# Loading the first convolution's taps 0 and 4 in alternating column halves, with a new written-out order for every engine

## The chip, the cores and the metric

The kernel runs on 1 core of one Trainium2 chip. The metric is the device time of one execution in microseconds, the median of the runs shown. PE is the matmul engine, PEld its weight load, DVE the vector engine, ACT the scalar engine, POOL GpSimd, SP the engine that issues nearly all DMAs.

## What is computed

Two convolutions over time with five taps, each followed by gelu and by keeping every second step, then a joint of the result with a short second sequence. Shapes: x is 2 x 4000 x 512, each tap is 512 x 512, g is 2 x 8 x 512, the output is 2 x 1000 x 8 x 512, all bf16.

```python
for i in range(5): h = h + einsum("btc,cd->btd", xp[:, i:i+T, :], w1[i])
h = gelu(h)[:, ::2, :]
for i in range(5): f = f + einsum("btc,cd->btd", hp[:, i:i+T1, :], w2[i])
f = gelu(f)[:, ::2, :]
fe = einsum("btd,de->bte", f, w_f);  ge = einsum("bud,de->bue", g, w_g)
j = tanh(fe[:, :, None, :] + ge[:, None, :, :])
out = einsum("btud,dv->btuv", j, w_o)
```

## The kernel before

**Stages.** The channels lie on the partitions in four blocks of 128. The first 396 steps of h are made by the plain method ("direct"): for each tap in the order 0, 4, 2, 1, 3 and each of four output blocks m, four matmuls of 396 columns add into bank m of PSUM, 80 matmuls in all. Their x comes by two ordinary loads (xr) and a transposition on PE; DVE and ACT copy the result to xs, rows 0 and 2 of a group of four first (taps 0, 4 and 2 need only these), rows 1 and 3 by a second pair of copies (taps 1 and 3). The rest of h, and all of f, is made by units (class Unit, steps s1 to s5; class Triple, steps d, r, t, s). A unit computes three output steps at a time with fewer products, from sums and differences of rows of x (tiles row and xq or xp, on DVE and ACT) and from sums of taps (w1part for the first convolution, w2part for the second). The x of the units comes by transposing DMAs. Then follow the feature product (class Feature) and the joint: tanh on ACT into jT and jX, and products with w_o in groups of four tiles (class Seven) with seven products of half size in place of eight, from sums of j (tile ss, on DVE or POOL) and of w_o (tile tw). Products are evicted by ACT or DVE to sn or og, added there, and stored by SP.

**The sums of taps.** w1part(m, "s") makes, for output block m (128 columns of each tap): t = w0 + w4, u = w0 + 4 w4, then u + 2 w2, t - w2 and t + w2, on DVE, the results scaled by 1/3 on ACT. For m = 0 and 2 it also makes the sum and the difference of taps 1 and 3 for two blocks at once. u goes into the product "t2", the first of a unit; t - w2 into "tm"; the difference of taps 1 and 3 into "sm". Blocks 0 and 1 lie in the first half of a tap's columns.

**The loads.** All on SP, in this order: the two xr; tap 0 as two column halves of 256 KB; taps 4, 2, 1 and 3 whole, 512 KB each. From tap 2 on, the issue of a load waits for the landing of an earlier one (list came): tap 2 for the first xr, tap 1 for the second, tap 3 for tap 0's second half. Then come the transposing loads of x: xq[0] in the phases 4, 0, 2, 1, 3, 5, then xq[1], then xp.

**The order.** The kernel is first recorded as a list of operations, numbered as they are recorded. ORDER gives for each engine the numbers of its operations in the order in which they are issued, two characters each. Some operations (evictions, sums in the joint and feature stages) can run on one of two engines ("flex"); the table in which the number stands decides. edges() works out which operation must wait for which; emit() issues each engine's list with the waits on semaphores. So the table, and not the order in the source, sets who runs before whom, and an engine waits at the first operation in its list that isn't ready.

**The old order's start, on DVE:** both copies to xs; u of block 1 and of block 0; t of block 0; the three operations that add tap 2 to these; then on in the same way through blocks 2 and 3, mixed with the row operations of the first units. The row difference for "t2" stands 11 places after the first operation that uses tap 2.

**The old order's end, on PE:** the first half of the last tile, the last product (p4) of the last group, the second half of the last tile. DVE evicts p4 and then the second half; ACT evicts the first half and issues both stores of the halves.

Of the kernel before, what the change touches and what calls it, by code (L numbers as in the profile page):

```python
# [63 lines left out]
class Op:  # L64
# [3 lines left out]
ALPHABET = "0123456789ABCDEFGHIJKLMNOPQRSTUVWXYZabcdefghijklmnopqrstuvwxyz_-"  # L68
ORDER = {
    "pe": (  # L70
        "0X0Y0Z0a0b0c0d0e0f0h0j0l0t0u0v0w0x0y0z0_0-1011121314151617182C2v191g1A2c2J1i1j2m2K2n2E2e2f2x2y2F2p362q372M2N33342j3O"
        "3P303J313K2k3H3X3t3U3R3S3h3i3Z4A3e3V3a3v3f413w3k3l4Y4K4L4244454o4a4C4D3_3-4b4N4i4y5L4l4O4H4j4m4v4I4z5V4f4q5p4w4r5N5W"
        "5O4g5z5_4-5r5s6L5S5T50606N6O6l616S6V5w6W5x7R6n6v6T6o5Y5Z6y6Y786Z6s6w7b7c7I7J7F6z7p7G6t7A837B7T7U7r7s7L7Y7M80817Z7z8A"
        "7_7e8D8T858E7f7w868V8d7x8e8W8B8m8a8t8r8b8n8-908u8g8h8o9F9G8G8H9Q9T8y8z8p9D9K929f9R9L9U939N9q9h9o9y9v9O9xA3ANA2A7A09j"
        "A9AiAjAEABAw9kAxAZAaAHAKB1AIALAfApAqAcB2BDAdAgBEB4B5BKBLBVAsAtB7BAB8BYBZBNBOBkBBBbBRBcBqBSBrBWBtBuC8BeBhBiBfCHC1CBC9"
        "ClCCCEC2CFBzCWCICTB_CUCaCXCbCmCoCpCrCKCLD5D6DFD2CuD3DJCsCeDKCvDVDBDCCfDWDSDTDPDQCxCyDuDMDnDNDcDoDdDjDkDvDfDgDxDyE4E5"
        "EEEZEFEaE1E2ETEUEOD_D-EPE_EtEuEBECEKELEfFCE-EcEdFDEWEXFOF4F2FFFGFWFXEwFxExFjFIFJFyFZFuFaFrFsFlFQFLFvFMGKFfFgGEGLGTG7"
        "GUG8F_F-GFG1GAGBGNGWGeGfGOGzGQGRGYGhGiGwGxH3GnHMH5GoHNH0GtGuG_HYHEH1HgHhHBHCHFHSHVHTHaHxI1HWHIHJI2HyHPHQHpIYHqH_H-IS"
        "IBICHjIxITHkI4IyIZIVI5IWIIIJIiIbIjJBIEIcIFJCJOJ1IlJPJ2I_I-ImJ4JRJ5IrJEIsJFJeJIJSJfJUJVJXJJJtJhJiJuJYJzJ_JwJxJnKMKNK0"
        "K7K8KAKEJoKFK1KPKBKcKVKdKQKSKWKTLKL0LLKzKfKwKtKgLQKxKuK_L1KlLRKmL7LTL8LaLbLALBLELpLFLNLULjLOLkLqMILyLzMOLsLtLvLdLeMJ"  # L80
        "MlM6MPLwM3M7M4MRMmMSMAMBMYMLMMMuMZMfM-MgN0MrNGMoMpMbMcMsNHMvNlNMNJNKN6NNN7N2N3NWNXNZNmNPOEOFNaNuNQNdNvN-O0NeNrNsOKOU"
        "NoOLONOVOnOHNpO6O7OhOOOiOoO2O3P8OIP9ObOkOxOyOcOXOqOYP2OlOrPBPEPCPZP3POPPO_O-PFPHPRPSPIPcQ0PdQ1PaPiPjPVPsPWPfPpPqQ9Pg"
        "PtQCQ3Q4QDPwPxQ6QAQ7QFQGQJQKQMQNQQQTQUQX"),
    "act": (
        "080k1o1s1L0m1N1R2S1Q1P1B1y2D1C1q1D1h2d1_1a1k2L2o1c1F2w2U1E2r2I2X2O353Q2W2Y2l383I2i3u3Y3B3T3N323j3p3D3W3n3g4B3o3m2-43"
        "4Z4M4S404p3d46545M3z4k4U4P4n534J4_4x525q654h5X4e5-4G6-516m6M5U5v67626X5y5a4u5K7S6U5R79705o6a717K6x6R7H6_7d6u5J7j5n6r"
        "847q7l7a7N6K6J7-8F7E828U7g5h6k8O6j7X8f7v897y8C8s6D8P918c8N976d8Z8x8I9J778i9E8q8_9M9S9V94999i9p9r9z9PA4ATAO9-A6AkAUAG"
        "ADAWAVAJAXC4AMB0A-AYBFCjB9Ba9nBPC7C6BXBlBvChCkCiCAC3C5CVDHDICnD7DGCODsDtDLD4CgA_FADXERCzESFoDeDwDhF8F9F6F7E6DrEQGJED"
        "EgEvFqFEFPFnF3FYFpEyGsFbFBINFmGrHtG9GIGCHuGgIMGXGjJrIQHOGvJMHvIvHDHiIPHzIOI3KqIRHlIUIzHwIwIaIkKLJDJ3InJsKKJGJNJgJWJj"
        "J-KIK9KpKrKCKeNjKULIKhKvK-LoL9NhLCKJLJNELrLnLfMKLxKsM8MnMHMaMGMjMtMdNIMkN4NCNYNnNbOGNFNDODOWOMNiOjNkOpOCOZPAOgOfP0PG"  # L90
        "PTPbQ2PrPhPuQEQ8QHQRQSQZ"),
    "dve": (
        "000g0i1m1J1I1n1M1K1O2Q1l1u2R1r1p1w1S1X1x1v1U1T1H1V1z1W1G1Y1Z1b1-1t2g1d2z2P2G2T2_2H1e1f2V2h2Z2b2a2t3L2s3M393q2u3C3A3b"
        "3E3F3c3x3G3r3s49474R3y4E4F4T4c484X4d4Q55574s4V564W5d4t5b665t5u5P645c5Q6b5G636A6P5k5E5f735H5F686p5g5I6Q5i5j696q5l6G72"
        "6C5m7Q6c6H746E7C6B7P7D7k7t7i7V7O7u6F6g7o7W7h6I766e6h756f877m7n886i8X8Y8k8Q8v8S8l8R9H9I8w9895968j9W9Y9a9g9c9X9Z9e9b9s"
        "9C9B9w9t9_9uA5A1A8AA9AARAFAC9l9mAyAPAbAzAQ9dAlASArB3AeAhB6BMBHBJAuBIBmBCBdBTBsBpBgBoC_CPCDBjCGB-CJCYCqCcCMCNCtCwE7Ep"
        "DZDDEqE8DREADUDODpDqDlDzErEhEiEGEbE3EVE0EnFSEmEMEeEYF0F5FHEoFVFkFzFKFtFRFNFhGMFwG0GVG2GGGPGSGZGyH8HcH4GpH6G-H2HZHGHU"
        "HbHKHXHRHrIDI0I8IfJ7I6IKIXIGJ8IgJQJ0IdJ6ItJTJaK4JbK6JKJvJyKOJZJpK2KGKRKXL4KaL6L-KbLMKyKnLSL2LcLGLVLPLlLuL_LZMWMUM2M5"
        "MQMxMCMNMhMTN1MqMwNLN8NONSNxNTOQNyNRNwO1NtNfNqO8NzO4OJOPOzOdOmPDP4PQOsPJPePLPlPMPmPNPXPkQ5PyQBQLQOQVQY"),
    "pool": (  # L100
        "01020304050n0o0p0q21200r0s5e8MAnAmBGAoBnCRC-D0CQCSDYDaD1EsDbEkE9EjFUFTElG3GaG4G5H9G6GbGcH7I7HAHdGdI9J9HeHfIeIhIAJAJc"
        "K3JdL3KYK5KZM0LWLXL5LYM1MVMXMyMzM_NUORNVOTN_OSOtOuOvOwPKPoPn"),
    "sp": (
        "0607090A0B0C0D0E0F0G0H0I0J0K0L0M0N0O0P0Q0R0S0T0U0V0W22232425262728292A2B58595A5B5C5D8J8K8LAvBQBUBwBxByC0CZCdD8D9DADE"
        "DiDmEHEIEJENEzF1FcFdFeFiGDGHGkGlGmGqHHHLHmHnHoHsIHILIoIpIqIuJHJLJkJlJmJqKDKHKiKjKkKoLDLHLgLhLiLmM9MDMEMFMeMiN5N9NANB"
        "NcNgO5O9OAOBOaOeP1P5P6P7PUPYPvPzP_P-QIQPQW"),
}


# [175 lines left out]
def bass_standalone__seq2seq_rnn_t_joint__speech_kernel(  # L285
# [19 lines left out]
    B, T, D = x.shape  # L305
# [15 lines left out]
    with ExitStack() as es:  # L321
        cur = [16512]

        def at(name, shape, dtype, offset=None):
            o = cur[0] if offset is None else offset
            b = Buf(nc, name, shape, dtype, o)
            if offset is None:
                cur[0] = (b.end + 31) // 32 * 32
            return b
# [3 lines left out]
        w1_sb = at("w1_sb", [K, NK, D], BF16)  # L333
# [52 lines left out]
        pl = Plan(nc)  # L386
# [42 lines left out]
        def load_w(eng, dst, src):  # L429
            return pl.dma(eng, lambda e: e.dma_start(dst.ap, src), (), (dst,))  # L430
# [3 lines left out]
        def load_xr(rt):  # L434
            n = NR[rt]
            dst = xr[rt].rows(0, n).map(lambda a: a.rearrange("p r k c -> p (r k c)"))
            src = x[0, 4 * P * rt:4 * (P * rt + n), :].rearrange("(p r) c -> p (r c)", r=4)
            return pl.dma("sp", lambda e: e.dma_start(dst.ap, src), (), (dst,), nbytes=n * 4 * 2 * D)  # L438

        def load_x6(buf, b, ph, j0, col, n=336):  # L440

            r0 = b * T + 6 * j0 + ph
            dst = buf[ph, :, col:col + n]
            src = x.rearrange("b t d -> (b t) d")[r0:r0 + 6 * (n - 1) + 1:6, :]
            pl.dma("sp", lambda e: e.dma_start_transpose(out=dst.ap, in_=src), (), (dst,), nbytes=n * 2 * D, rate=172e3)

        came = [load_xr(rt) for rt in range(2)]
        act(warm[0:1], warm[1:2], ACT.Gelu_apprx_tanh)

        def load_w1(i):  # L450
            src = w1[i].rearrange("(k c) d -> c k d", c=P)
            if len(came) == 2:
                h = D // 2
                for sl in (slice(0, h), slice(h, D)):
                    o = pl.dma("sp", lambda e, sl=sl: e.dma_start(w1_sb[i, :, sl].ap, src[:, :, sl]), (), (w1_sb[i, :, sl],), nbytes=262144)  # L455
            else:
                o = load_w("sp", w1_sb[i], src)
                if len(came) > 3:
                    o.after.append(came[-4].idx)
            came.append(o)  # L460

        def load_xq(i, ph):
            load_x6(xq[i], 0, ph, 2 * NA // 3 + i * N3 - 2, 0, -(-(N3 + 3 - i) // 16) * 16)

        for kind, i in (('w', 0), ('w', 4), ('w', 2), ('w', 1), ('w', 3), ('x', 4), ('x', 0), ('x', 2), ('x', 1), ('x', 3), ('x', 5)):
            if kind == "w":
                load_w1(i)
            else:
                load_xq(0, i)
        for ph in (4, 0, 2, 1, 3, 5):  # L470
            load_xq(1, ph)
        for ph in (4, 0, 2, 1, 3, 5):
# [10 lines left out]
        for rt in range(2):  # L483
            for pp in range(2):
# [9 lines left out]
                o = xs[0][pp::2, :, 16 + rt * P:16 + rt * P + n]  # L494
# [187 lines left out]
        for m in range(NK):  # L682
            src = ps.pair(m * NT, NA, NA).map(lambda a: a.rearrange("p s (q r) -> p s r q", r=3))
            o = hT[0][:, m, HOFF:HOFF + NA // 3].map(lambda a: a.rearrange("p (r s) q -> p s r q", s=2))
# [516 lines left out]
```

## Time and profile before

| | us |
|---|---|
| median of 3 runs (250.22 to 250.87) | 250.55 |
| the profiled execution: device time | 250.92 |
| the profiled execution: span, first to last instruction | 249.10 |
| busy: PE, DVE, ACT, POOL | 242.8, 225.0, 210.4, 86.5 |
| first matmul of the 80 direct ones | 7.21 |
| first sum of taps on DVE | 9.48 |
| last matmuls begin | 244.94 |
| granted TensorE clock, mean | 1.000 |

The span is shorter than the device time by 1.82 us, which lie outside of the program's instructions. A row of the timeline is: start, time that the merged instructions span, engine, line, operation, output and inputs, shapes, count, and in brackets the idle time of the engine before it with what ended it. Matmuls overlap: one of 268 columns is shown with 0.28 us, but the next begins 0.115 us after it. Idle time of PE is therefore read from the starts. A row of the table by stretch is: stretch, length, busy time of PE, PEld, DVE, ACT and POOL with the number of instructions, granted clock, busy share of the DMA engines and GB/s.

### The profile page before, as it was taken

The numbers are of one execution on the slowest core, as the hardware profiler recorded it, in microseconds if no ns is written. First come the engines' busy times: TensorE is split into PE (matmuls) and PEld (weight loads), VectorE is DVE, ScalarE is ACT, GpSimd is POOL, SyncE is SP. The second block draws the span as 40 slices with busy tenths as digits, with TensorE's granted clock in tenths as the row PEclk, the third lists the DMA queues.
The fourth block names the chain that finished last, engine by engine and source line by source line (L and its number), as shares of the span: only waits on it lengthen the run. The fifth ranks groups of instructions, "written<-read, shape, count | busy, mean of one in ns | idle before, by whom it ended". The sixth has DMA issues, their size and how long they took to land.

```text
span 249.1 us, 5276 instructions
## 1 busy us (share of the span) xinstructions
PE 242.8 (97%) x1932; PEld 184.2 (74%) x1932; DVE 225.0 (90%) x399; ACT 210.4 (84%) x359; POOL 86.5 (35%) x92
## 2 busy tenths in 40 slices
PE   7999999999999999999999999999999999999994
PEld 3556888877666666666568887878778888888783
DVE  1599988984999999799999898999999999999994
ACT  2198699859765957996999999999999999999972
POOL 1000000000000000000015494677987796787850
PEclk9999999999999999999999999999999999999999
DMA  7999999985700620000000533223323665446557
GB/s 194 340 190 167 203 174 202 167 130 168 234 21 3 184 69 3 0 3 3 0 0 3 168 101 112 84 88 127 132 87 105 201 199 171 141 157 206 168 183 227
DMA packets 57323, 31.85 MB, mean 128 GB/s; under 512 B 33786, under 2 KB 57098, under 8 KB 57298
## 3 DMA queue, kind: packets, MB, share of 16 engines
q1 hardware_dynamic: 57010, 31.39, 48.0%
q8 instruction: 15, 0.25, 0.4%
q10 hardware_dynamic: 288, 0.13, 0.2%
q14 instruction: 10, 0.08, 0.1%
HBM read 7.64 MB, written 16.38 MB: 96 GB/s over the span
## 4 chain that ended last, share of the span: by engine, by line
PE 87%; DVE 7%; DMA 3%; issue 1%; SPq 1%; DVEq 0%
PE acc L412 87%; DMA w_sb<-in_w_dram 3%; DVE ssum L502 2%; DVE row L398 2%; DVE ssum L398 1%; DVE og L818 1%; DVE og L398 1%; DVE w_t L398 0%; SPq L455 0%; SPq L438 0%; DVE ss L886 0%; DVEq L321 0%; DVE w_x L398 0%; DVEq L246 0%
## 5 line engine op out<-in xcount | busy, mean ns | idle before, releaser
L398 DVE TENSOR_TENSOR og<-acc,sn 128x512 bf16<-128x512 f32 x93 | 59.6, 682 | 1.9 <-PE acc L412 1.6
L412 PE MATMUL acc<-tw,ss 128*128 128x256 f16 x372 | 57.6, 273 | 0.1
L404 ACT ACTIVATE jT<-feT,geT 128x1000 bf16<-128x1000 f32 (+6 forms) x56 | 52.1, 982 | 0.1
L817 ACT ACTIVATE sn<-acc 128x512 f32<-128x512 f32 (+1 forms) x67 | 41.3, 666 | 1.7 <-PE acc L412 1.6
L412 PEld LDWEIGHTS acc<-tw,ss 128*128 128x128 f16 x372 | 35.8, 98 | 6.4 <-DVE ss L886 0.4
L886 POOL TENSOR_TENSOR ss<-jT 128x512 f16<-128x512 bf16 x25 | 28.8, 1163 | 24.5 <-ACT jT L404 24.5
L412 PE MATMUL acc<-row,w_sb 128*128 128x334 bf16 (+1 forms) x192 | 32.0, 296 | 0.0
L412 PE MATMUL acc<-row,w_x 128*128 128x268 bf16 (+1 forms) x192 | 28.8, 291 | 0.5 <-ACT sd L404 0.4
L412 PE MATMUL acc<-wo_sb,jT 128*128 128x256 bf16 x176 | 28.9, 272 | 0.0
L404 ACT ACTIVATE sd<-acc 128x334 f32<-128x334 f32 (+1 forms) x48 | 20.1, 432 | 9.4 <-PE acc L412 7.3
L394 POOL MEMSET hT<- 128x8 bf16 (+2 forms) x6 | 0.7, 147 | 77.1 <-ACT hT L404 72.2
L404 ACT ACTIVATE jX<-feT,geT 128x1000 bf16<-128x1000 f32 (+4 forms) x28 | 27.0, 999 | 0.1
L412 PEld LDWEIGHTS acc<-row,w_x 128*128 128x128 bf16 x192 | 18.5, 98 | 6.9 <-ACT sd L404 0.7
L412 PEld LDWEIGHTS acc<-row,w_sb 128*128 128x128 bf16 x192 | 18.5, 98 | 6.5 <-DVE row L398 0.2
L412 PE MATMUL acc<-wo_sb,ss 128*128 128x256 bf16 x124 | 21.4, 273 | 0.0
L404 ACT ACTIVATE hT<-acc 128x268 bf16<-128x268 f32 (+2 forms) x36 | 15.0, 436 | 6.1 <-PE acc L412 6.1
L412 PEld LDWEIGHTS acc<-wo_sb,jT 128*128 128x128 bf16 x176 | 17.2, 98 | 2.9
L818 DVE COPY sn<-acc 128x512 f32<-128x512 f32 (+1 forms) x28 | 18.7, 679 | 0.1
L886 POOL TENSOR_TENSOR ss<-ss,jT 128x512 f16<-128x512 f16 x11 | 13.4, 1221 | 12.7 <-DVE ss L886 10.0
L412 PE MATMUL acc<-row,w_t 128*128 128x334 bf16 x96 | 17.0, 305 | 0.0
L817 ACT ACTIVATE og<-acc 128x512 bf16<-128x512 f32 x25 | 16.7, 668 | 0.2 <-PE acc L412 0.2
L412 PE MATMUL acc<-hT,w_sb 128*128 128x334 bf16 x96 | 16.8, 305 | 0.0
(115 smaller groups left out, 499.9 us busy)
## 6 DMA issues: line engine op xcount, KB each, us to landing
out_dram<-og SPq DMA_DIRECT2D x47, 256.0 KB, 2.3
w_sb<-in_w_dram SPq DMA_DIRECT2D x9, 512.0 KB, 5.9
out_dram<-og SPq DMA_DIRECT2D x15, 128.0 KB, 2.4
xr<-in_x_dram SPq DMA_DIRECT2D x1, 512.0 KB, 4.0
w_sb<-in_w_dram SPq DMA_DIRECT2D x2, 256.0 KB, 5.5
wf_sb<-in_w_f_dram SPq DMA_DIRECT2D x1, 512.0 KB, 3.6
wg_sb<-in_w_g_dram SPq DMA_DIRECT2D x1, 512.0 KB, 4.7
wo_sb<-in_w_o_dram SPq DMA_DIRECT2D x1, 512.0 KB, 5.7
```

Source lines behind the costliest of these rows:

```text
L394: pl.op("pool", lambda e: e.memset(v.ap, 0.0), (), (v,))
L398: pl.op(eng, lambda e: e.tensor_tensor(out=o.ap, in0=a.ap, in1=b.ap, op=op), (a, b), (o,), 0.02 + 2.14e-3 * o.ap.free_size() if eng == "po ...
L404: pl.op("act", lambda e: e.activation(o.ap, i.ap, func, scale=scale, bias=0.0 if bias is None else bias.ap), rd, (o,), o.ap.free_size() * ...
L412: ins = e.matmul(o.ap, lhsT=l.ap, rhs=r.ap, start=start and n == 0, stop=stop and n == len(pairs) - 1, skip_group_check=not check)
L502: pl.op(eng, lambda e: e.scalar_tensor_tensor(out=o.ap, in0=a.ap, scalar=f, in1=b.ap, op0=ALU.mult, op1=add), (a, b), (o,), vec_cost(o, (a ...
L817: pl.flex({"act": (lambda e: e.activation(o.ap, v.ap, ACT.Copy), 0.05 + n * 0.833e-3), "dve": (lambda e: e.tensor_copy(out=o.ap, in_=v.ap) ...
L818: "dve": (lambda e: e.tensor_copy(out=o.ap, in_=v.ap), 0.065 + n * 1.04e-3)}, (v,), (o,))
L886: fn = lambda e, o=S[i], x=x, y=y, op=op: e.tensor_tensor(out=o.ap, in0=x.ap, in1=y.ap, op=op)
```

## The change

It has two parts. The first changes the loads: tap 4 is loaded in column halves too, and the halves of taps 0 and 4 alternate: first half of 0, first half of 4, second half of 0, second half of 4. The first three are issued at once; the second half of tap 4 waits for the landing of the first xr, tap 2 for the second xr, tap 1 for the first half of tap 4, tap 3 for the second half of tap 4. So one operation is added, and all numbers behind it go up by one.

```diff
-        def load_w1(i):
+        def load_w1(i, h=None, gate=None):
             src = w1[i].rearrange("(k c) d -> c k d", c=P)
-            if len(came) == 2:
-                h = D // 2
-                for sl in (slice(0, h), slice(h, D)):
-                    o = pl.dma("sp", lambda e, sl=sl: e.dma_start(w1_sb[i, :, sl].ap, src[:, :, sl]), (), (w1_sb[i, :, sl],), nbytes=262144)
+            if h is None:
+                o = load_w("sp", w1_sb[i], src)
             else:
-                o = load_w("sp", w1_sb[i], src)
-                if len(came) > 3:
-                    o.after.append(came[-4].idx)
+                sl = slice(h * D // 2, (h + 1) * D // 2)
+                o = pl.dma("sp", lambda e: e.dma_start(w1_sb[i, :, sl].ap, src[:, :, sl]), (), (w1_sb[i, :, sl],), nbytes=262144)
+            if gate is not None:
+                o.after.append(came[gate].idx)
             came.append(o)
...
-        for kind, i in (('w', 0), ('w', 4), ('w', 2), ('w', 1), ('w', 3), ('x', 4), ('x', 0), ('x', 2), ('x', 1), ('x', 3), ('x', 5)):
-            if kind == "w":
-                load_w1(i)
-            else:
-                load_xq(0, i)
+        for i, h, gate in ((0, 0, None), (4, 0, None), (0, 1, None), (4, 1, 0), (2, None, 1), (1, None, 3), (3, None, 5)):
+            load_w1(i, h, gate)
+        for ph in (4, 0, 2, 1, 3, 5):
+            load_xq(0, ph)
```

The second part replaces all five tables of ORDER. The operations are the same but for the added load. What the new tables do:

- **DVE at the start:** the first xs copy; t of block 0, u of block 0, u of block 1; the second xs copy; then the operations that use tap 2. The row difference for "t2" now stands 12 places after the first of these.
- **PE at the start:** the 80 direct matmuls in the same order, but the first four products "t2" stand after 68 of them and not after 72. The direct matmuls of tap 0 wait for its first half, and after eight for its second; so do those of tap 4.
- **Flex operations:** 69 stand on another engine than before. In sum ACT has three more, POOL two more and DVE five fewer.
- **The end:** on PE the last group's p4 comes behind both halves of the last tile. ACT evicts the first half and p4, DVE the second half.
- **SP:** the same stores, some of them in another order.

More of the change, by code (lines that the diff above doesn't have):

```diff
@@ L70 @@
     "pe": (
[L71 to L82, printed above, removed]
@@ L83 @@
-        "PtQCQ3Q4QDPwPxQ6QAQ7QFQGQJQKQMQNQQQTQUQX"),
-    "act": (
[L85 to L91, printed above, removed]
@@ L92 @@
-    "dve": (
[L93 to L99, printed above, removed]
+        "0Y0Z0a0b0c0d0e0f0g0i0k0m0u0v0w0x0y0z0_0-1011121314151617182D191h2d1A2w1B2K2L2n2o1j1k2f2g2F2G2y2z2q2r2N37382O34353P2k"
@@ new lines @@
+        "3Q313K2l3I323L3Y3u3V3i3j3W3S3f3T423w3a3b433x4Z4B4D4E4L3-3g45464M3l3m4b4c4O404I4p4g4m5M4J4j4k4P4n4w4x5W4z4r4_5q5X4s4h"
+        "5O5P5T5U505s6M515_5Z5t5-6m6W6X5a6O6w6x6P6T5x5y7B796U61626o6p7J7K6Z7C7U6t7S6z6a7G7c7q7M6u7V7d7H7N6_7Z7s7t7f7g8U7a7_84"
+        "817-827x8B8C8E7y86878F8n8e8o8s8W8H8X8f8b8I8u8v908p8q919E8h8z8c8_9G9H9L939R8i9S9M9U9V949g9O9p9P9r9i9w9zA49yA1A8AAAOA3"
+        "9kAF9lAjAkAaAbACAIB2AxAyAJALB3AgBEAhBWBFAqAdArBXAeB8B9BZBLBMAMB5BaB6BlAtAuBcBdBSBTBrBBBOBsBCBPCIBfBuBvCCCFCGBgC9CAC2"
@@ new lines @@
+        "CDC3CmCUBiCJBjCVCLB_B-CbCpCqCXCYCnCcCMD6D7CsCvCtDGDKCfDLCwD3CgD4DWDdDCCyDeDXDNDODDDQDyDRDvCzDzDoDwDkDgDhDlDpDTDUEFEC"
+        "EDE5EUE6E2D-EVE3EPE0EQEaEbEGEgELEuE-EvEMFDEXEYEdEeFEF0FPF3ExFGFHEyF5FJFsFtFkFXFyFRFMFYFKFaFbFzFNG8G9FvFwGLFgFhFmGMG2"
+        "GBGCGFF-GGG0GUGOGZGVGRGSGfGuGgGPGXGoGvH1GiGpH4GjGxH2H6GyG_HZG-HNHCHyHTHOHzHDHUHFHGHbHhHiHQHWHXHqHRIZHrHJH-I0HKI2I3IC"
+        "HkHlITIaIyIDI5IUIJI6IzIKIcIWIFIjIXIGIkJ2J3IdJPImJCJQJDIsJ5I-ItInJ0JJJ6JSJKJTJuJvJfJYJFJgJVJGJiJjJWJ_JZK8J-K9JxK1K2KN"
@@ new lines @@
+        "JyKTKUKOJoKFKWKGJpKXK_KQKBKCKdKeLLKmKRKuKvLRK-LMKnKxKgKhLSL8L9L1LFL2KyLULbLqLVLcLGLrLOLPLkLBLCMPLlMQMJMKLtM4LeLfM5Lz"
+        "LuL_LwMmLxMnMZMaMMMSM7MNMBM8MTMCMpMsMtMqMgMhNHN0MvMcN1NIMdMwNmN3N4N7NKN8NNNLNnNONQNXNYOFNROGNaNsNeNfNbNvO0O1NtNpNqNw"
+        "OVOWOLOMOOOiO3OjO4OPOIOJOoOyOzOpOrO7O8OsOlOmOcOYPCOdOZPFP9PAPGPDP3P4PIPaO-P0PbPSPPPQPJQ1PTQ2PjPkPgPdPhPePqPrPWPXQDQE"
+        "PtQ4Q5PuPxPyQ7Q8QGQKQLQHQAQBQNQOQRQYQUQV"),
+    "act": (
+        "080l1M0n1p1O1z1S1r1R2T1Q2E1i2e1t1-1C1D1b2p2M1l1d1E1G2x1F2V392P2s2Y362X3R2Z2j2m3J3Z2J3v3C3k3o3U3E3X3330444C3p3q3h3O4N"
+        "4a473n4T413e4q5N4l4Q3_4V4K4o544-5Y554i535r4v4y4H526N66604f6n5V706y5L6Y5b5S686V5w5K7A5z5p7L636S727T6b715o6L6v7e7I5i7O"
+        "7k6s6-7r7w857h7Y6l7F807m8D7b6K838V7z8G8O8t8P6E8g6k8Q8J988A6e8a78929F8d8j9K8r8-9T9A959N9W8y9q9h9Q9j9_A59sAUA0APA7AVCk"
+        "AlAHAEAWCiAKAYAXAZBGAsB1BNANBAC7B0C5BYBmBtC6BwA-CBClC4DJCWCjC8CZDICoDtDHDMDuD5F9ChETESDY9oC_FpDiFBCPF7F8FADsE7EEERFr"
+        "EHEhEwGKFFFQF4EzFoFqGtGsFZFcFCHvGAFnHuG3INGJIwGhGYIRH5GkGwJNHwHPHEIQHHHxH_IPJsKrI4ISIEIVIxI_IOIbIlKsJEJRIoLoJOJwJhJk"
+        "JtJXKLKAKVKJKqKKKfKMKwNiL0KiLTLALJLKLsLdMkMLLpM6KtLyMoMbMHM9MuMIMlMeNJNFNkNDNPN5NoNZOHNcNENlOXNjO5NGO_OhODOaOEPBOgP1"
+        "PRPcPHQ3PUPsPiQFPvQ9QIQSQTQWQa"),
@@ new lines @@
+    "dve": (
+        "000h1J1K1n0j1L1P1o1x1N1y1m1v1q2R1I2S1T1s1V1w1U1_1W1X1H1Y1Z1a1c1u202h1e2H2Q2_2U2-1f2I1g2i2W2u2a2c2b3M2t3N2v3D3A3B3r3c"
+        "3F3d3G3y3z3s3H4F4G3t49484d4R4U4e4A4S4X564Y4W4t4u585d5e5Q57645c5F5u655H5I675v5R6B746c5l5G6Q6A5m5J6R6q6r6C6H69737D6I7E"
+        "5j6D5h7R5k5g5n7Q757P7W7X6F6d6h7u7l7v6i776G7j6J7i6f7p887n6g897o6j8R8T8Y8S768w8Z8m8l978x96999I9X9b9J8k9f9Y9d9a9Z9B9t9u"
+        "9x9v9-A29eABA6A99CAG9mAcAD9n9DAzA_B4AiAoAmAnATBHBpBIApAfBbB7AvBeBnBUBQBDBqC-CQBhCECHCKBkC0CrCdCNCODZDaEAD8CuEqDbCxDf"
+        "DEDPDSD_DxDmDqDVEBDrEiEjElEWE4E1EcEnFTEoENEZF1EfFIF6EpFlFuFSFLFOF_FxFiGNGDGHG1GaGTGQI8HAH9HdGWGqH7GzH0HaH3HVHcHjHYHS"
+        "HsHLI1HmI9IgJ8I7ILIYIHJ9IhJ4IeIuJ1J7JUJbK5JcJHJLJaK0K3JzKPKHJqKYKDKSKbL5M0KcLNKoLXL7KzLWLHLQLDL3LmLgLvL-MyM2MVM3MRMD"
+        "MOMiMrN2MUMxN9NMNTNyNVNUORNzNSNgNrO2NxOkNuONOKOQO9OqOeOnPEP5OtPNOxPLPmPMPKPfPlPYQ6PzQMQCQPQZ"),
@@ L100 @@
     "pool": (
-        "01020304050n0o0p0q21200r0s5e8MAnAmBGAoBnCRC-D0CQCSDYDaD1EsDbEkE9EjFUFTElG3GaG4G5H9G6GbGcH7I7HAHdGdI9J9HeHfIeIhIAJAJc"
-        "K3JdL3KYK5KZM0LWLXL5LYM1MVMXMyMzM_NUORNVOTN_OSOtOuOvOwPKPoPn"),
+        "010203040522210o0p0q0r0s0t5f8N9cASBJAQARBKCSBoD0D2CRD1CTDcErE8EsEtE9EkG4FUEmFWGbG6G5GcFVH8G7GdHeGeHgHBJAIAHfIfIiIBJB"
+        "JdK4K7JeKZL4KaK6M1LYL6LZLaMXMWMzMYM_M-OSN_NWOTN-OuOUOvOwPnPOPoPp"),
     "sp": (
-        "0607090A0B0C0D0E0F0G0H0I0J0K0L0M0N0O0P0Q0R0S0T0U0V0W22232425262728292A2B58595A5B5C5D8J8K8LAvBQBUBwBxByC0CZCdD8D9DADE"
@@ L105 @@
-        "DiDmEHEIEJENEzF1FcFdFeFiGDGHGkGlGmGqHHHLHmHnHoHsIHILIoIpIqIuJHJLJkJlJmJqKDKHKiKjKkKoLDLHLgLhLiLmM9MDMEMFMeMiN5N9NANB"
-        "NcNgO5O9OAOBOaOeP1P5P6P7PUPYPvPzP_P-QIQPQW"),
+        "0607090A0B0C0D0E0F0G0H0I0J0K0L0M0N0O0P0Q0R0S0T0U0V0W0X232425262728292A2B2C595A5B5C5D5E8K8L8MAwBRBVBxByBzC1CaCeD9DADB"
+        "DFDjDnEIEJEKEOE_F2FdFeFfFjGEGIGlGmGnGrHIHMHnHoHpHtIIIMIpIqIrIvJIJMJlJmJnJrKEKIKjKkKlKpLELILhLiLjLnMAMEMFMGMfMjN6NANB"
+        "NCNdNhO6OAOBOCObOfP2P6P7P8PVPZPwP_P-Q0QJQQQX"),
 }
```

## The prediction

> **What bounds the kernel now.** All durations below are from the one profiled execution: span 249.10 us, device time 250.92 us, so 1.82 us lie around the span; the runs shown have a median of 250.55 us, 0.37 us below that execution. I work out a difference in the span and put it on the median.
>
> I read the page first, then the chain of waits that ended last in order of time:
>
> ```profile
> PE 242.8 (97%) x1932; PEld 184.2 (74%) x1932; DVE 225.0 (90%) x399; ACT 210.4 (84%) x359; POOL 86.5 (35%) x92
> ```
>
> ```profile
> 2.65 6.81 DMA w_sb<-in_w_dram
> ...
> 9.48 1.29 DVE ssum L502 x2
> ...
> 24.24 201.41 PE acc L412 x1614
> ```
>
> PE is the bound from 24.24 us on; 201 us of matmuls follow without a piece of another engine between them. Ahead of it stand tap 4's load, issued at 2.65 and landed at 9.46 (2.65 + 6.81), and then DVE without a pause. So only idle time of PE can be won. For it I went to the timeline. Where matmuls run freely, four of 268 columns start 0.46 us apart, which is 0.115 each; one of 396 columns takes 0.1675, one of 256 columns 0.11.
>
> ```profile
> 22.04 0.62 PE L412 MATMUL acc<-row,w_x 128*128 128x268 bf16 x4
> ...
> 23.10 3.14 PE L412 MATMUL acc<-row,w_x 128*128 128x268 bf16 x24 [0.44 <-ACT sd L404]
> ...
> 24.24 1.71 PEld L412 LDWEIGHTS acc<-row,w_x 128*128 128x128 bf16 x16 [0.35 <-DVE row L398]
> ```
>
> Four matmuls from 22.04 take 0.46, the next start at 23.10: 0.60 us lost. Eight from 23.10 take 0.92, the next start at 24.24: 0.22 lost. **The start loses 0.82 us.** Then the end:
>
> ```profile
> 225.27 0.38 PE L412 MATMUL acc<-wo_sb,jX 128*128 128x256 bf16 x2
> ...
> 225.67 0.61 PE L412 MATMUL acc<-tw,ss 128*128 128x256 f16 x4
> ...
> 231.14 0.38 PE L412 MATMUL acc<-wo_sb,ss 128*128 128x256 bf16 x2
> ...
> 231.64 0.83 PE L412 MATMUL acc<-tw,ss 128*128 128x256 f16 x6
> ```
>
> The starts are 0.40 and 0.50 apart where two matmuls need 0.22; with 232.30 to 232.84 (0.32 lost) and 243.98 to 244.50 (0.08) **the end loses 0.86 us**. Everything that a new order can win by closing waits is therefore about 1.7 us.
>
> Last, what DVE does ahead of 24.24, and how fast loads run:
>
> ```profile
> 9.48 1.29 DVE L502 SCALAR_TENSOR_TENSOR ssum<-w_sb 128x512 f32<-128x512 bf16 x2 [2.72 <-DMA w_sb<-in_w_dram]
> 10.70 0.68 DVE L398 TENSOR_TENSOR ssum<-w_sb 128x512 f32<-128x512 bf16 x1
> 11.30 0.68 DVE L502 SCALAR_TENSOR_TENSOR ssum<-w_sb,ssum 128x512 f32<-128x512 bf16 x1
> ...
> 17.92 0.71 DVE L398 TENSOR_TENSOR row<-xq 128x1072 bf16<-128x1072 bf16 x1
> ```
>
> ```profile
> 5.20:6.20 1.00, 0.85 (x18) 0.68 (x16) 0.72 (x2) 0.00 (x0) 0.00 (x0) 1.00 1.23 282
> 8.00:12.00 4.00, 4.00 (x26) 2.30 (x24) 2.52 (x5) 0.00 (x0) 0.00 (x0) 1.00 1.09 350
> ```
>
> DVE starts a weight sum each 0.60 us and a row operation each 0.63. The last figure of a window is GB/s: 282 while column halves (rows of 512 B) are moved, 350 while whole taps are. A half of 262 kB takes 0.93 us at the one rate, 0.75 at the other; the two halves of tap 0 landed 1.20 us apart (issued at 1.66 and 2.10, landing 5.1 and 5.9 us later: 6.76 and 7.96).
>
> **The loads.** One DMA is added (tap 4 becomes two halves), its issue 0.4 us on SP, beside waiting. The queue is now 0a, 4a, 0b, 4b, 2, 1, 3. 4a takes 0b's place: 7.96. 0b follows 0.93 later: 8.89; 4b 9.82. Tap 2 landed at 10.97 (issued 4.79, 6.2 later); the halves of tap 4 take 0.36 us more than the whole did (2 x 0.93 less 1.50), so 11.33. Bounds from the rows: 0.75 each (0b 8.71, tap 2 10.97) and 1.20 each (0b 9.16, tap 2 11.87).
>
> By the Trainium skill, DMA: Bandwidth & Descriptors, Specifications, rows of 512 B and more move at line rate. By that rule tap 2 stays at 10.97; the trace disagrees, 282 against 350 GB/s.
>
> **A new wait on PE.** The 16 matmuls of tap 0 begin at 7.21, behind ACT's copy of xs, which nothing here moves. The first eight end at 7.21 + 8 x 0.1675 = 8.55; before, 0b was there at 7.96. Now it comes at 8.89, and a landing is followed 0.05 later (xr at 4.77, PE at 4.82): **0.39 us lost**, bounds 0.21 and 0.66. All of PE's queue stands behind it. 4b, tap 2 and the others are needed at 11 us and later, and are in time.
>
> **The sums on DVE.** They begin at 7.98 and no longer at 9.48. But after three of them the new order has the second xs copy (0.65, no longer in the idle time ahead) and then an operation that needs tap 2. DVE is there at 7.98 + 1.80 + 0.65 = 10.43 and waits until 11.35. In the old order the first operation with tap 2 ran at 11.30. **So most of the 1.5 us is given back at the next load**; only the order behind it counts. Twelve operations on (7.22 us) stands the row difference for the first 268-column products: 18.57, readable 0.68 later at 19.25. PE comes to it after 68 matmuls of 396 columns: 7.21 + 0.39 + 11.39 = 18.99, and loses 0.26. Then 12 x 0.1675 + 16 x 0.115 = 3.85 to the next kind of product: 23.10; its row is six operations (3.69) later at 22.26, readable 22.94: no wait. The one after it is readable at 23.57, PE is there at 23.56. Lost in the start: 0.39 + 0.26 = 0.65 against 0.82, **-0.17 us**. With the bounds: 0b 8.71 and tap 2 10.97 give 0.29 (-0.53); 0b 9.16 and tap 2 11.87 give 1.19 (+0.37).
>
> **SP behind the loads.** Tap 3's load waits for 4b and is issued at 9.82 where it was 7.98; twelve transposes are queued behind it, first at 10.25 and not 8.39. The first landed 0.91 after tap 3, so about 15.2, in time for ACT, which is at 15.7 when it wants it. The second landed at 17.28; DVE wants it at 18.57. If it slips in full (1.86) it lands at 19.14, and the start costs 0.57 more; unobstructed transposes land 4.7 after their issue, by which it would be 16.3 to 18. I take no cost. Later ones follow in a train about 1.5 us apart whose readers come microseconds later.
>
> **The new order elsewhere.** The same matmuls run. Of the operations that may change engine, ACT takes and gives nearly equal numbers; in the stretch 200 to 225 it takes five evictions from DVE and gives four:
>
> ```profile
> 175.00:200.00 25.00, 25.00 (x217) 20.84 (x216) 24.80 (x47) 25.00 (x40) 20.54 (x19) 1.00 0.43 140
> 200.00:225.00 25.00, 25.00 (x231) 22.08 (x229) 24.74 (x48) 25.00 (x43) 19.61 (x17) 1.00 0.51 165
> ```
>
> PE, DVE, ACT (first, third and fourth count) are all full, so one more eviction at 0.48 us costs 0 (taken up earlier, where 125 to 175 has some room) to 0.48; I take 0.2. Waits in this stretch can't be read off from before: bounds 0 and one long tanh, 1.02 us. For the end I take the same 0.86, bounds 0 and twice that. The last product now comes behind the last half tile; its eviction on ACT (0.6), issue and landing (2.4) replace DVE's copies and the same landing: under 0.1 us.
>
> **Sum:** -0.17 + 0.2 = +0.03 us: 250.6, no change that a measurement of this kernel can tell (about 0.3%, 0.75 us).
>
> **Rivals.** *Faster:* halves move at line rate, as the skill's rule has it, so the start wins 0.53, and the new order closes half of the end's waits (0.43): 249.6; with all of them 249.2. For it: DVE is one unbroken chain up to 24 us, so each tenth that tap 2 is earlier counts. Against it: 282 GB/s. *Slower:* in 175 to 225 one eviction that returns a bank stands behind one more tanh of 1000 columns (1.02 us); with eight banks all turning, PE stops at the next product. It decides as soon as the eviction is over 0.3 us later than its bank is wanted, since ACT has no idle time to catch up. 1.02 less 0.17: 251.4; two such, 252.4. For it: ACT at 25.00 of 25.00. Against it: the old order, as full, has no break there. *Start only:* transposes slip in full, +0.4: 251.0, inside the first case's bounds.
>
> **Chances.** No change 0.43, faster 0.25, slower 0.32. The range 249.3 to 251.9 takes in the faster case and one lost tanh, and leaves out some 0.1 on each side.
>
> **What would show it.** PE idle near 8.55 for 0.2 to 0.7 us, ended by the second half of tap 0; DVE sums from about 8.0 and then idle until tap 2 lands near 11.3; a short wait near 19; PE unbroken until 225. Wrong if tap 2 lands by 11.0, if the second transpose lands after 18.6, or if PE loses over 0.5 us in 125 to 225.

## The result, and the profile after

| | before | changed |
|---|---|---|
| median of 6 runs each, same chip (us) | 250.56 (250.22 to 251.64) | 249.29 (249.07 to 249.52) |
| ratio, with its 95% interval | | 0.9944 (0.9924 to 0.9963) |
| the profiled execution: device time, span (us) | 250.92, 249.10 | 249.07, 247.27 |
| PE's first direct matmul | 7.21 | 6.88 |
| idle time of PE, from the matmul starts: start, 30 to 225, end | 0.85, 0.41, 0.86 | 0.60, 0.06, 0.03 |

The changed kernel is faster by 1.27 us between the medians (the ratio of the runs is 0.9944). The forecast was no change. The idle times are summed from the starts, less the usual step of each kind of matmul; they are good to about 0.03 us.

The line of the page that counts the engines, in the changed kernel:

```profile
PE 241.8 (98%) x1932; PEld 185.6 (75%) x1932; DVE 222.9 (90%) x394; ACT 212.0 (86%) x362; POOL 88.7 (36%) x94
```

The same 1932 matmuls run; DVE is busy 2.1 us less and ACT 1.6 us more. The chain of waits that ended last, in order of time (start, length, what):

```profile
4.35 4.78 DMA w_sb<-in_w_dram
...
10.97 6.08 DMA xq<-in_x_dram
17.05 0.02 issue
17.07 1.10 ACT row L404
18.18 0.54 ACT w_x L404
18.71 0.10 issue
18.82 224.06 PE acc L412 x1816
242.88 0.02 issue
242.90 0.39 ACT ost L815
```

In this chain PE is now one piece from 18.82 to 242.88; before, the long piece began at 24.24 and broke at 225.65. So the gain at the end can be seen at once. What went on in the start is in the timeline (start, time, engine, line, operation, shapes, count; in brackets the idle time before it and what ended it):

```profile
7.38 0.69 DVE L398 TENSOR_TENSOR ssum<-w_sb 128x512 f32<-128x512 bf16 x1 [1.46 <-DMA w_sb<-in_w_dram]
8.00 1.28 DVE L500 SCALAR_TENSOR_TENSOR ssum<-w_sb 128x512 f32<-128x512 bf16 x2
8.31 9.87 PEld L412 LDWEIGHTS acc<-xs,w_sb 128*128 128x128 bf16 x60 [0.30 <-DMA w_sb<-in_w_dram]
9.20 0.68 DVE L496 COPY xs<-acc 128x1024 bf16<-128x1024 bf16 x1
10.73 0.69 DVE L500 SCALAR_TENSOR_TENSOR ssum<-w_sb,ssum 128x512 f32<-128x512 bf16 x1 [0.85 <-DMA w_sb<-in_w_dram]
...
17.96 0.71 DVE L398 TENSOR_TENSOR row<-xq 128x1072 bf16<-128x1072 bf16 x1
...
18.82 0.62 PE L412 MATMUL acc<-row,w_x 128*128 128x268 bf16 x4 [0.24 <-ACT w_x L404]
```

DVE's sums start at 7.38 and no longer at 9.48. But three sums and one copy later DVE stands for 0.85 us, until tap 2 is there at 10.63. PE loses 0.07 us at 8.31 (second half of tap 0), 0.41 at 18.82 and 0.12 at 27.37. The bracket at 18.82 names ACT, but the product there needs the row difference on DVE (17.96, result at 18.67): the weight that it takes was made by an operation of ACT long before. A releaser is inferred from which semaphore came last, and the ACT operation that ended at 18.70 happened to be that: the operation that these four matmuls wait for on ACT is the one at 12.66.

At the end, the waits of PE's weight loads from 222 us on (who waits, for whom: us in total, times, longest), before:

```profile
PEld acc L412 <- DVE og L398: 0.6, 2, 0.4
PEld acc L412 <- DVE ss L886: 0.4, 1, 0.4
PEld acc L412 <- ACT sn L817: 0.3, 1, 0.3
```

In the changed kernel the same view from 222 us on has no row at all.

The accounts of the two executions: 0.25 us from the start, 0.35 from 30 to 225, 0.83 from the end, and 0.33 because PE began earlier (7.21 less 6.88) make 1.76 of the 1.83 us between the spans. The medians differ by 1.27 only. The difference lies in the choice of executions: the profiled one of before stood 0.36 above its median, the changed one 0.22 below. So the 0.33 can't be put down to the change, and the experiments show how much the start varies by itself.

### The profile page after: what moved, and what is told of

Read it like the earlier page. It is cut to its first block, busy times and chain, and to the rows that moved or that the text cites. A ratio compares the mean times of both kernels' runs of the same rounds, so it can differ in the third digit from the quotient of the medians.

```text
span 247.3 us, 5295 instructions
## 1 busy us (share of the span) xinstructions
PE 241.8 (98%) x1932; PEld 185.6 (75%) x1932; DVE 222.9 (90%) x394; ACT 212.0 (86%) x362; POOL 88.7 (36%) x94
## 4 chain that ended last, share of the span: by engine, by line
PE 91%; DMA 6%; ACT 1%; SPq 1%; ACTq 0%; issue 0%
PE acc L412 91%; DMA xq<-in_x_dram 2%; DMA w_sb<-in_w_dram 2%; DMA xr<-in_x_dram 1%; SPq L445 1%; ACT row L404 0%; ACT og L815 0%; ACT w_x L404 0%; ACTq L830 0%; ACT ost L815 0%; SPq L430 0%; ACTq L246 0%
## 5 line engine op out<-in xcount | busy, mean ns | idle before, releaser
L404 ACT ACTIVATE jT<-feT,geT 128x1000 bf16<-128x1000 f32 (+6 forms) x56 | 54.3, 1017 | 0.3
L815 ACT ACTIVATE sn<-acc 128x512 f32<-128x512 f32 (+1 forms) x73 | 46.5, 725 | 0.7 <-PE acc L412 0.5
L412 PEld LDWEIGHTS acc<-tw,ss 128*128 128x128 f16 x372 | 36.3, 98 | 6.1
L884 POOL TENSOR_TENSOR ss<-jT 128x512 f16<-128x512 bf16 x22 | 25.6, 1174 | 13.9 <-ACT jT L404 13.4
L404 ACT ACTIVATE jX<-feT,geT 128x1000 bf16<-128x1000 f32 (+4 forms) x28 | 27.5, 1048 | 0.3 <-PE acc L412 0.3
L884 POOL TENSOR_TENSOR ss<-ss,jT 128x512 f16<-128x512 f16 x14 | 17.1, 1228 | 10.0 <-DVE ss L884 8.2
L884 POOL TENSOR_TENSOR ss<-jT,ss 128x512 f16<-128x512 bf16 x13 | 15.4, 1186 | 6.8 <-DVE ss L884 5.5
L815 ACT ACTIVATE og<-acc 128x512 bf16<-128x512 f32 x22 | 16.1, 731 | 0.9 <-PE acc L412 0.8
```

The lines of the kernel that those rows point to most:

```text
L404: pl.op("act", lambda e: e.activation(o.ap, i.ap, func, scale=scale, bias=0.0 if bias is None else bias.ap), rd, (o,), o.ap.free_size() * ...
L412: ins = e.matmul(o.ap, lhsT=l.ap, rhs=r.ap, start=start and n == 0, stop=stop and n == len(pairs) - 1, skip_group_check=not check)
L815: pl.flex({"act": (lambda e: e.activation(o.ap, v.ap, ACT.Copy), 0.05 + n * 0.833e-3), "dve": (lambda e: e.tensor_copy(out=o.ap, in_=v.ap) ...
L884: fn = lambda e, o=S[i], x=x, y=y, op=op: e.tensor_tensor(out=o.ap, in0=x.ap, in1=y.ap, op=op)
```

## The experiments

Two theories at first. **Loads:** the early halves let the sums and so the first products start sooner, and the gain is made before 30 us. **Rest:** the loads give nothing that lasts; the gain is made by the order behind the start, above all at the end. Each kernel below is compared with the kernel before on the same chip; its median there was 250.34, 250.30 and 250.25 us in the three groups of four.

### First group: the two parts alone, and the order cut at 40 us

**loads_alone**: the new loads, the order of before. Its tables hold the old places, with the numbers from tap 4 on raised by one and the added half in SP's table.

> The new loads with the old tables of order (numbers moved up by one; the added half tap stands in SP's list where the new tables have it). Theory 1 (most of the 1.27 us comes from the new order away from the start): the three first sums are done before tap 2 lands, so DVE's chain starts at tap 2's landing and not after it; PE loses 0.4 to 0.7 in the start where before it lost 0.82, and keeps the 0.86 of the end: 0.1 to 0.4 us faster than before, 250.2 to 250.45. Theory 2 (the loads bring the gain, the new order only follows them): about 249.4.

Measured: 250.47 us, ratio 1.000 (0.9991 to 1.0008). By the medians the loads alone move nothing; theory 1 had 0.1 to 0.4 us. DVE's timeline:

```profile
6.92 1.29 DVE L500 SCALAR_TENSOR_TENSOR ssum<-w_sb 128x512 f32<-128x512 bf16 x2
8.13 0.69 DVE L398 TENSOR_TENSOR ssum<-w_sb 128x512 f32<-128x512 bf16 x1
10.29 0.69 DVE L500 SCALAR_TENSOR_TENSOR ssum<-w_sb,ssum 128x512 f32<-128x512 bf16 x1 [1.47 <-DMA w_sb<-in_w_dram]
```

Three sums run early, and most of the advance is then given back in a wait of 1.47 us for tap 2. This profile is of the fastest of eleven executions (249.98 us): tap 2 landed at 10.19 and not at 10.97 as in the profile of before, and PE lost nothing in the start. The median lies 0.49 us above it, so the usual execution does not keep that; where it loses it, no profile shows.

**order_alone**: the old loads, the new order.

> The new tables with the old loads (tap 4 whole, tap 0's halves one after the other). DVE's sums then begin at tap 4's landing near 9.5, with the second xs copy still among them, so DVE reaches its first operation with tap 2 near 11.9 where the changed kernel reached it at 10.73. Theory 1: PE loses 1.2 to 1.7 us in the start and next to nothing at the end: 250.2 to 250.8, close to before. Theory 2 (the start decides): it has the cost of the start and no gain elsewhere: 251.3 or more.

Measured: 249.90 us, ratio 0.9983 (0.9971 to 0.9994). Faster by 0.4 us, a third of the gain, and better than either theory had it. Its profile loses 0.8 us of PE up to 30 us (0.69 of it at 19.04) and 0.35 at 37.36 and 38.07. The next kernel differs from it only in the order up to 40 us and is 1.07 us faster on the same chip: without the early halves the new order of the start costs about 1 us. That is not yet a gain by them.

**old_start_new_rest**: the old loads; what began before 40 us in the kernel before keeps its engine and its place, all that comes later stands as in the new tables.

> Old loads; operations that began before 40 us in the profile of before keep their old order and engine, all later ones have the new order. Theory 1: the start keeps its 0.82 us of lost time, the waits after it go: 0.9 to 1.2 us faster than before, 249.3 to 249.7. Theory 2: as before, 250.4 to 250.7.

Measured: 248.83 us, ratio 0.9942 (0.993 to 0.9954). It is 1.51 us faster, the whole gain and a little more than theory 1 had, without one of the new loads. The theory of the loads falls here.

**new_start_old_rest**: the reverse, the new loads and the new order up to 40 us, the old order behind.

> New loads; operations that began before 40 us in the profile of the changed kernel keep the new order, all later ones have the old order. Theory 1: the start gains about 0.2 us, the end loses its 0.86 again: 250.2 to 250.5. Theory 2: as the changed kernel, 249.2 to 249.5.

Measured: 251.46 us, ratio 1.0041 (1.0029 to 1.0053). Slower; but in its profile PE waits 0.65 us at 40.7 and 0.36 at 44.2, where the two orders were joined, which makes up 1.01 of the 1.1 us. That lies outside of both theories, and so near the joint it says little of the start's worth.

### Second group: what in the rest

In the end of the kernel before, one row stands out. Timeline of before, DVE and POOL:

```profile
230.15 1.43 DVE L886 TENSOR_TENSOR ss<-jX 128x512 f16<-128x512 bf16 x1
...
230.15 1.15 POOL L886 TENSOR_TENSOR ss<-jX 128x512 f16<-128x512 bf16 x1
...
231.50 0.68 DVE L818 CAST og<-acc 128x512 bf16<-128x512 f32 x1
```

DVE takes 0.41 us for such a sum elsewhere. Here it starts in the same moment as one on POOL and ends 0.28 us behind it: it has stood until POOL was through. The eviction and the add behind it on DVE come 1.0 us later for it, and PE waits at 231.64 and 232.84. The same row has 1.43 us in loads_alone (229.22) and in new_start_old_rest (230.54): it belongs to the old order. The new tables put this very sum (operation 1533, with the added load 1534) on POOL, where it runs well before the other one of the pair, 1564, which begins at 227.98:

```profile
225.75 1.16 POOL L884 TENSOR_TENSOR ss<-jX 128x512 f16<-128x512 bf16 x1
```

None of the 52 sums into ss on DVE in the changed kernel begins while POOL sums; those that overlap one were begun 0.15 us or more ahead of it.

**one_wait**: the kernel before, with one dependence more: POOL's sum (operation 1564) follows DVE's (1533).

```diff
+        pl.ops[1564].after.append(1533)
```

> The kernel before with one wait added: the POOL sum that began at 230.15 us in the profile waits for the DVE sum that began in the same moment and took 1.43 us where others of its kind take 0.41. The POOL sum's result is first read at 234.2, so the wait itself costs nothing. Theory A (two of the end's waits on PE, 0.28 and 0.32 us, come from this one long DVE operation): DVE's sum takes 0.41, and the kernel is 0.5 to 0.65 us faster than before. Theory B (they come from the places of evictions and adds in the lists): no change, within 0.15 us.

Measured: 249.75 us, ratio 0.9974 (0.9958 to 0.999). Its timeline:

```profile
229.66 0.41 DVE L886 TENSOR_TENSOR ss<-jX 128x512 f16<-128x512 bf16 x1
230.16 1.16 POOL L886 TENSOR_TENSOR ss<-jX 128x512 f16<-128x512 bf16 x1 [0.45 <-DVE ss L886]
230.20 0.69 DVE L818 CAST og<-acc 128x512 bf16<-128x512 f32 x1
```

DVE's sum takes 0.41 again, POOL's begins 0.45 us later than it could, and the kernel wins 0.55 us. This one collision is so worth nearly half as much as the whole change; two waits of PE stay at the end (from the starts 0.19 us at 225.19 and 0.08 at 243.40).

**new_middle_old_end**: as old_start_new_rest up to 215 us, the old order behind.

> Old loads, old order up to 40 us, new order up to 215 us, old order again for all operations that began after 215 us. Theory 1 (the end is the largest part of the gain): 0.8 to 0.9 us slower than old_start_new_rest, which was 1.45 us faster than before: so 0.5 to 0.7 us faster than before. If the middle were the larger part, it would be within 0.3 us of old_start_new_rest. The seam at 215 us can cost something by itself, where an operation that the new order had moved to another engine meets the old order of the rest.

Measured: 249.90 us, ratio 0.9992 (0.9971 to 1.0014). Inconclusive: behind the joint PE waits 0.74 us in its profile (0.34 at 217.07 and 0.40 at 219.06, both for evictions on ACT), which is as much as either theory was to show. One thing can be read from it: DVE's sum stands on DVE there as before, but it begins at 229.75, 0.90 us into a sum of POOL, and takes 0.54 us and not 1.43; from 225 us on PE then loses 0.08 us and not 0.86. That fits the collision as the cause of that loss, though the waits at the joint had also given DVE and ACT time to catch up.

**halves_not_alternated**: the changed kernel with tap 0's halves first.

```diff
-        for i, h, gate in ((0, 0, None), (4, 0, None), (0, 1, None), (4, 1, 0), (2, None, 1), (1, None, 3), (3, None, 5)):
+        for i, h, gate in ((0, 0, None), (0, 1, None), (4, 0, None), (4, 1, 0), (2, None, 1), (1, None, 3), (3, None, 5)):
```

> The changed kernel, with the two halves of tap 0 loaded first and then the two of tap 4; all else is the same. Theory 1 (early sums gain nothing, since DVE then waits for tap 2): DVE begins 0.9 us later, ends three sums and a copy just as tap 2 lands, and PE no longer waits for tap 0's second half: within 0.2 us of the changed kernel, 0.4 to 0.65 % faster than before. Theory 2 (sums from halves of both taps are worth their time): 0.5 to 0.9 us slower than the changed kernel.

Measured: 249.25 us, ratio 0.9949 (0.9929 to 0.997), not to be told from the changed kernel. DVE's timeline:

```profile
8.24 0.69 DVE L398 TENSOR_TENSOR ssum<-w_sb 128x512 f32<-128x512 bf16 x1 [2.27 <-DMA w_sb<-in_w_dram]
8.85 1.29 DVE L500 SCALAR_TENSOR_TENSOR ssum<-w_sb 128x512 f32<-128x512 bf16 x2
10.05 0.68 DVE L496 COPY xs<-acc 128x1024 bf16<-128x1024 bf16 x1
10.69 0.69 DVE L500 SCALAR_TENSOR_TENSOR ssum<-w_sb,ssum 128x512 f32<-128x512 bf16 x1
```

The first sum starts 0.86 us later than in the changed kernel, and the first sum with tap 2 at the same time (10.69 against 10.73), now without a wait. To alternate the halves moves idle time of DVE, no more.

**new_loads_old_start_new_rest**: as old_start_new_rest, but with the new loads.

> The kernel old_start_new_rest with the new loads in place of the old ones; the order up to 40 us stays the old one, the rest the new one. In the old order DVE has both xs copies behind it when tap 4's first half lands, and three sums before tap 2. Theory 1 (the loads are worth nothing): within 0.2 us of old_start_new_rest, so 0.5 to 0.65 % faster than before. Theory 2: the loads gain 0.4 to 0.7 us with the order that suits them: 0.75 to 0.85 % faster than before.

Measured: 249.16 us, ratio 0.995 (0.9933 to 0.9966). With the old order of the start the loads make no difference either.

### Third group: the end by itself, a use for the early halves, and repeats

**old_to_225_new_end**: the old loads, the old order up to 225 us, the new one behind.

> Old loads; operations that began before 225 us in the profile of before keep the old order and engine, the later ones have the new order. At 225 the two orders have nearly the same operations behind them, so the seam should be cheaper than the one at 215. Theory 1 (the waits of the last 20 us are the larger part of the gain, 0.86 us): 0.75 to 0.95 us faster than before. If the small waits between 50 and 225 us were the larger part: 0 to 0.4 us faster.

Measured: 249.44 us, ratio 0.9962 (0.994 to 0.9983): 0.81 us faster by the new end alone. Its chain in order of time:

```profile
7.68 235.65 PE acc L412 x1884
243.33 0.02 issue
243.35 0.39 ACT ost L817
```

PE is unbroken to 243.33. one_wait won 0.55 of it; the other 0.26 fit the two waits that it left at the end (0.19 and 0.08), as far as medians from two chips can be set against each other.

**five_sums_first**: if DVE stands 0.85 us until tap 2 comes, sums that need none of it could stand there. new_loads_old_start_new_rest, with the sums u of blocks 2 and 3 right behind the first three, in buffers of their own.

```diff
+        us = [ssum[2], ssum[3]] + [Buf(nc, f"us{i}", [NK, P], FP32, w2_sb.end - 4096 + 2048 * i) for i in range(2)]
...
-                t, v, u = ssum[4][:], ssum[m % 2][:], ssum[2 + m % 2][:]
+                t, v, u = ssum[4][:], ssum[m % 2][:], us[m][:]
```

> new_loads_old_start_new_rest with buffers of their own for the sums of the blocks 2 and 3 (4 KB in a part of the second convolution's weights that is not yet in use), and with these two first sums moved up on DVE: five sums that need taps 0 and 4 alone stand ahead of the first that needs tap 2, where three stood. Theory 1 (the early halves are worth nothing only because DVE has nothing more to do until tap 2 lands): DVE's wait for tap 2, 1.4 us, is filled with 1.2 us of work that is then missing later; PE's waits near 19 to 25 us go, 0.2 to 0.6 us faster than new_loads_old_start_new_rest, 0.6 to 0.75 % faster than before. If the start is bound by something else (xr's landing, the transposes): no difference, 0.5 % faster than before.

Measured: 249.15 us, ratio 0.9958 (0.9946 to 0.997). No gain over 249.16 without it (on another chip, by the ratios 0.9958 against 0.995): the second case of the expectation. DVE's timeline:

```profile
9.07 1.28 DVE L500 SCALAR_TENSOR_TENSOR us<-w_sb 128x512 f32<-128x512 bf16 x2
10.59 0.69 DVE L500 SCALAR_TENSOR_TENSOR ssum<-w_sb,ssum 128x512 f32<-128x512 bf16 x1 [0.24 <-DMA w_sb<-in_w_dram]
...
14.20 0.69 DVE L398 TENSOR_TENSOR w_x<-w_sb 128x1024 bf16<-128x1024 bf16 x1 [0.38 <-DMA w_sb<-in_w_dram]
```

The wait for tap 2 shrinks to 0.24, and DVE then arrives early at the sum that needs tap 3, which landed at 14.17, and waits 0.38 there. In this execution the loads bound DVE, not the place of the sums.

**old_start_again** and **changed_again**: old_start_new_rest and the changed kernel once more, on one chip.

> The same kernel as old_start_new_rest, beside the others of this call. Theory 1: as before or up to 0.4 us faster than the changed kernel; 0.5 to 0.65 % faster than before.

> The changed kernel itself, beside the others of this call: 0.4 to 0.6 % faster than before.

Measured: 249.07 us, ratio 0.9952 (0.994 to 0.9964), and 249.22 us, ratio 0.9956 (0.9944 to 0.9968). The two can't be told apart: the first part of the change, loads and order of the start together, is worth nothing that these runs can see against the old loads and the old start. PE's timelines of the two, first of old_start_again:

```profile
4.34 1.58 PE L491 MATMUL acc<-ident,xr 128*128 128x128 bf16 x32
...
6.64 12.27 PE L412 MATMUL acc<-xs,w_sb 128*128 128x396 bf16 x72 [0.73 <-DMA w_sb<-in_w_dram]
...
21.45 0.62 PE L412 MATMUL acc<-row,w_x 128*128 128x268 bf16 x4
...
22.83 3.14 PE L412 MATMUL acc<-row,w_x 128*128 128x268 bf16 x24 [0.75 <-DVE row L398]
```

and of changed_again:

```profile
4.58 2.82 PE L489 MATMUL acc<-ident,xr 128*128 128x128 bf16 x32
...
7.71 11.61 PE L412 MATMUL acc<-xs,w_sb 128*128 128x396 bf16 x68 [0.32 <-ACT xs L404]
...
23.00 2.90 PE L412 MATMUL acc<-row,w_x 128*128 128x268 bf16 x24
```

Where PE begins early (6.64) it waits later (0.75 at 22.83), where it begins late (7.71) it does not, and both are at their first 24 products together near 23 us. One profile of the start can show either; that is why the start's 0.25 us between the two profiles shown at the top can't be called a gain.

## Why the prediction was wrong, point by point

The sign and the size of the forecast (+0.03 us, in effect none) were wrong; what it said of the loads and the start was right in the main, and what it said of the rest was wrong.

- **Loads: right in kind, too late by 0.4 us in this profile.** Halves landed 0.86 to 0.91 us apart (forecast 0.93). Tap 2 came 4.15 us behind the first half of tap 0, where the forecast was 4.57 and the profile of before has 4.21; it landed at 10.63, and "tap 2 lands by 11.0" was one of the prediction's own signs of being wrong. Most of the miss is one number: it took 1.20 us between two landings from the profile of before, and the two that were issued first landed 0.88 apart. Over all profiles that 1.20 is unusual: of the seven profiles with the old loads five have 0.82 to 0.98. There tap 2 came 3.81 to 4.31 us behind the first half, 3.94 in the middle; in the seven with the new loads it came 4.15 to 4.19 behind. So by the middle values the split does delay tap 2, by some 0.2 us (forecast 0.36), and this one pair of profiles hides it. Rows of 512 B moved at 294 GB/s (5.20 to 8.50), whole taps at 345 (the last figure of these windows; 9.20 to 12.00 is the other):

```profile
5.20:8.50 3.30, 2.75 (x34) 1.66 (x32) 1.81 (x3) 0.65 (x1) 0.00 (x0) 1.00 1.20 294
9.20:12.00 2.80, 2.80 (x18) 1.63 (x17) 1.95 (x5) 0.55 (x2) 0.00 (x0) 1.00 1.09 345
```

The Trainium skill's rule that the prediction weighed (DMA: Bandwidth & Descriptors, Specifications) had tap 2 no later than before. In this pair of profiles so it came, but over the fourteen it did not, and the halves moved more slowly than the whole taps: the traces do not bear the rule out here.

- **The new wait on PE: mechanism right, too large.** 0.07 us against 0.39. The second half of tap 0 came 1.39 us behind PE's first direct matmul (8.27 less 6.88), not 1.68 (8.89 less 7.21). That is below the forecast's lower bound of 0.21.
- **The sums: right.** DVE starts at 7.38 (forecast 7.98; all of the start came 0.3 to 0.6 earlier in this execution), gives most of the advance back at tap 2, and PE waits near 19: 0.41 us, forecast 0.26. The start loses 0.60, forecast 0.65. By the medians of loads_alone and old_start_again nothing of it lasts.
- **SP's transposes: right.** The second landed at 17.05, and DVE wanted it at 17.96.
- **The order elsewhere: wrong.** +0.2 us was taken for one more eviction on ACT. ACT is busy 1.6 us more, but PE's waits from 30 to 225 fell from 0.41 to 0.06 us. Two pairs of experiments agree with that: old_to_225_new_end, with the old order there, loses 0.41 us in its profile, and old_start_new_rest and old_start_again, with the new one, lose less than 0.01 each. In time, old_start_again is 0.37 us faster than old_to_225_new_end on one chip, but the intervals of their ratios overlap. What the slower rival went by, ACT without a gap from 175 to 225 us (the fourth count of these windows of the changed kernel), is still there and stops no product:

```profile
175.00:200.00 25.00, 25.00 (x221) 21.28 (x219) 24.95 (x48) 25.00 (x41) 19.98 (x19) 1.00 0.43 138
200.00:225.00 25.00, 25.00 (x232) 22.40 (x230) 24.93 (x49) 25.00 (x43) 18.49 (x17) 1.00 0.52 169
```

- **"For the end I take the same 0.86": the step that failed.** The end lost 0.03 us in the changed kernel, and the new order there is worth 0.81 by old_to_225_new_end. The prediction had half of these waits in its faster rival, at 249.6, and all of them at 249.2; the time came out there, but with nothing from the loads, which that rival began with. It carried the end's four waits over to the new order as they were. A look at what stood behind one of them would have shown otherwise: the weight load at 231.63 waits for a DVE sum, and that sum took 1.43 us where its kin take 0.41. A row that is three times as long as the others of its form is not a cost of the work. The tables that the prediction had before it put this sum on POOL, so that the two could no longer meet; one_wait took the collision away with one line, and that alone is 0.55 of the 0.81. The other two waits of the four (0.19 and 0.08) were not tried one by one.

What stays open: how the new order closes the small waits between 30 and 225 us (the longest, 0.14 us at 125.46, stood behind an add on DVE), since no kernel changes them one by one; and what the usual execution of loads_alone loses.

## What to carry to other kernels

Before a wait is put down as fixed, look at the duration of the operation that ends it against other rows of its form: here an outlier marked a collision, and one dependence between two operations removed it, as did the new tables by moving one of the two to the other's engine. An advance that is won at one load counts only as far as the next load's landing; follow it to the first operation that needs that one. A change of several parts is worth what its parts are worth on the chip: here the loads it was named for won nothing over the old start and only paid for what the new order of the start costs without them, and the best version run, the old loads and start with the new order behind (0.9942 and 0.9952), can't be told from the whole change.

## What the runs showed of the hardware

- A sum of two SBUF tiles on DVE and one on POOL hold each other up. Started in the same moment (230.15), DVE took 1.43 us for 0.41, POOL its usual 1.15. Started 0.8 us into a POOL sum (154.86; the POOL sum ran to 155.35), DVE took 0.77. Where POOL started 0.03 us ahead of DVE (217.38 and 217.41, before), it was POOL that took 1.46, and DVE kept 0.41:

```profile
217.38 1.46 POOL L886 TENSOR_TENSOR ss<-jX,ss 128x512 f16<-128x512 bf16 x1
217.41 0.41 DVE L886 TENSOR_TENSOR ss<-jX 128x512 f16<-128x512 bf16 x1
```

  With starts this near to each other the records don't tell who will stand: in loads_alone POOL was recorded 0.01 us ahead (229.21 and 229.22), and it was DVE that stood. Begun 0.15 us or more ahead, DVE kept its 0.41 in every case, and POOL's sum took 1.27. The Trainium skill, SBUF — State Buffer, Who interferes with whom, says that a VectorE instruction with two inputs in SBUF contends with a GpSimd one that reads SBUF, and that the order of issue decides which of the two is blocked. The traces agree that one stands for the other, in both directions. In these cases the delay is a little less than what was left of the other: 1.02 us of 1.15, 0.36 of 0.49, 0.31 of 0.39, and 0.12 of 0.25 where DVE was 0.16 ahead. That it is always the later one, the records can't show: at 217.38 the one with the earlier start stood.
- PE's first matmuls run at half the later rate, up to a moment that differs from execution to execution. In all 14 profiles the matmuls of 512 columns ahead of the transposes begin 0.40 to 0.43 us apart, where matmuls of 504 columns later begin 0.213 apart. The transposes of 128 columns begin 0.107 apart up to the time at which the profile's first record of the granted clock begins, and 0.056 apart behind it; that time lies between 4.1 us (old_start_again) and 7.2 (changed_again), which is why the 32 transposes span 1.58 us in the one and 2.82 in the other. The table by stretch gives a clock of 1.00 for both, since there is no record for the time before.
- With this and the landings of x, PE's first direct matmul comes at 6.64 to 7.71 us over the 14 profiles, and for the changed kernel alone at 6.88 and 7.71. The time of the whole kernel does not follow: these two took 249.07 and 249.22 us. Who begins early mostly waits for the loads later.
